# Moving stores to GpSimd's queue, reordering one unit's q loads and changing one PSUM bank in a fused attention and feed-forward kernel

## The chip, the cores and the metric

The kernel runs on one core of a Trainium2 chip (trn2). The metric is the device time of the core in microseconds. Several executions are timed for each kernel, and one of them is traced by the hardware profiler. Engines are named TensorE (PE in the profile, PEld for its weight loads), VectorE (DVE), ScalarE (ACT), GpSimd (POOL) and SyncE (SP, which computes nothing here and only issues DMAs; its queue is SPq). A wait of TensorE is given as its idle time, unless it is said to be counted from start to start. The granted clock is the share of TensorE's full clock that the profile says it was given. A bank is a buffer in PSUM, where the program has the results of matmuls written.

## The reference

```python
def _attn_ref(q, k, v, g_norm):              # (8, 8, 576, 64) each, float32
    kv = np.einsum('bhsd,bhse->bhde', k, v)
    out = np.einsum('bhsd,bhde->bhse', q, kv)
    rms = np.sqrt(np.mean(out * out, axis=-1, keepdims=True) + 1e-06)
    return (out / rms * g_norm).astype(np.float32)
# (B, H, S, D) -> x of (4608, 512), then
def _moe_ref(x, w_in, w_out, s, b):          # w_in (512, 2048), w_out (2048, 512)
    h = x @ w_in
    r = np.maximum(h, 0.0)
    g = s * (r * r) + b
    return (g @ w_out).astype(np.float32)
```

## The kernel before

The 4608 tokens are cut into 36 chunks of 128, and four chunks make a unit: unit `u`, from 0 to 8, has the chunks `4 * u` to `4 * u + 3`. Both large products use a seven-product scheme instead of eight plain ones, for the second product on two levels. While unit `u` is in its first product, the attention of unit `u + 1` is slipped in between: `turn` (transpose q), `product` (q times kv), `row_sum`, `norm`, `turn_x`. Each engine keeps the order in which the program issues its work, so the place of every call matters.

SyncE issues almost every DMA: loads of q, k and v, loads of w_out and its sums into a ring of seven buffers (`pump`), stores of the output, and, in unit 1, 42 stores of parts of w_out (18 as they are, 24 sums or differences), which later units load.

```python
        def parts_of_w(i):                        # unit 1 only, for six of the seven products
            ...
            sub(t1, y12, y11)
            sub(t2, y22, t1)
            sub(t3, y22, y12)
            sub(t4, y21, t2)
            for n, t in enumerate((y11, y21, t2, t3, t1, y22, t4)):
                nc.sync.dma_start(out=w3_dram[i][:, n], in_=t)

        def store(name, j, c, cols=slice(0, DM), queues=(nc.sync, nc.sync)):
            ...                                    # 2 to 4 DMAs a chunk

        def product(with_sum=True):               # q times kv
            ...
                pool, tag = (ps_f, "y") if c == 17 or c > 19 and c % 2 else (ps_a, "x")
                ps = pool.tile([P, NP, P], FP32, name="x_ps", tag=tag)   # ps_a has one buffer, "y" two
```

What unit 3 does for unit 4 (chunks 16 to 19), and the loads of q for chunks 22 and 23 that it issues; keys are (step, place) in the first product, and names of places in the second. `loads_in_parts(5, 1, 4)` cuts the 48 loads of these two chunks into four quarters of twelve.

```python
                first[2, 0] = [*turn_x[:2], turn[2]]
                parts = loads_in_parts(5, 1, 4)
                second["q", 0], second["q", 2] = [parts[2]], [parts[3]]
                first.update({
                    (2, 1): [product[2]],
                    (2, 2): [turn[3], row_sum[2], norm[2], *parts[:2]],
                    (2, 3): [turn_x[2]],
                    (3, 0): [product[3], row_sum[3]],
                    (3, 1): [norm[3]],
                    ...
                })
```

## Time and profile before

| | before |
|---|---|
| time, median of 3 runs | 953.4 us (952.8 to 954.4) |
| span of the traced run | 949.7 us |
| TensorE busy | 931.7 us |
| VectorE, ScalarE, GpSimd busy | 657.3, 204.8, 6.7 us |
| TensorE's named waits, all together | 11.4 us |
| last matmul's end to the end | 5.9 us |

TensorE is busy for nearly the whole span, so only its idle time can be saved.

### The profile page before, as it was taken

To read this page: it belongs to the slowest core of one execution; us is meant where nothing else is said; L and a number is where in the kernel's file an instruction comes from. 1 tells how busy PE (TensorE), PEld (TensorE's weight loads), DVE (VectorE), ACT (ScalarE), POOL (GpSimd) and SP (SyncE) were. 2 spreads that over 40 slices of the span, in tenths; PEclk is the share of its full clock that TensorE was granted. 3 is DMA by queue.
4 is the path that set the end of the run, shared out by engine and by line. 5 is a ranking of instruction groups with operands and counts; after the bars stand their busy time and mean duration, and the time that the engine had idled before them with its cause. 6 is when DMAs were issued, how large, how long until landed. Compare 5 with 4: busy or idle time off the path is not lost.

```text
span 949.7 us, 18256 instructions
## 1 busy us (share of the span) xinstructions
PE 931.7 (98%) x7438; PEld 841.1 (89%) x7438; DVE 657.3 (69%) x1220; ACT 204.8 (22%) x387; POOL 6.7 (1%) x18
## 2 busy tenths in 40 slices
PE   7999999999999999999999999999999999999997
PEld 7888888888888998899879998999889988998997
DVE  2799667486557775777477766776578757774585
ACT  3683132101223012300232013200320033001200
POOL 2000000000000000000000000000000000000000
PEclk9999999999999999999999999999999999999999
DMA  9689727578764767156744774277526720673075
GB/s 262 200 303 255 244 79 197 137 226 255 209 178 121 236 189 230 23 185 214 195 115 127 247 210 108 67 249 216 156 42 222 223 99 12 202 224 118 12 232 168
DMA packets 141220, 165.85 MB, mean 175 GB/s; under 512 B 78161, under 2 KB 94289, under 8 KB 141009
## 3 DMA queue, kind: packets, MB, share of 16 engines
q1 hardware_dynamic: 137072, 162.12, 57.1%
q10 hardware_dynamic: 3744, 2.56, 1.1%
q8 instruction: 59, 0.97, 0.4%
q14 instruction: 25, 0.20, 0.1%
q0 software_dynamic: 320, 0.00, 0.0%
HBM read 136.84 MB, written 27.79 MB: 173 GB/s over the span
## 4 chain that ended last, share of the span: by engine, by line
PE 83%; DVE 6%; DMA 5%; ACT 2%; SPq 2%; issue 1%; DVEq 0%; ACTq 0%
PE x_ps L91 36%; PE y_ps L91 26%; PE z_ps L91 9%; PE t_ps L91 7%; PE x_ps L440 3%; DMA w_sb<-w 2%; PE kv_ps L377 1%; ACT xT L494 1%; DMA w_raw<-in_moe_w_in_dram 1%; SPq L1261 1%; DMA kv_sb<-in_k_dram 1%; DVE a L247 1%; DVE xT L488 1%; DVE a L551 1%; DVE a L637 1%
## 5 line engine op out<-in xcount | busy, mean ns | idle before, releaser
L596 ACT COPY r<-x_ps 128x512 f32<-128x512 f32 x96 | 56.0, 583 | 398.0 <-PE x_ps L91 373.1
L91 PE MATMUL y_ps<-xs,wb 128*128 128x256 f32 x512 | 122.6, 382 | 1.1 <-DVE a L247 1.1
L91 PE MATMUL x_ps<-xs,ws 128*128 128x256 f32 x512 | 122.0, 381 | 0.5
L91 PEld LDWEIGHTS y_ps<-xs,wb 128*128 128x128 f32 x512 | 95.5, 190 | 16.9 <-DVE a L247 3.4
L91 PEld LDWEIGHTS x_ps<-xs,ws 128*128 128x128 f32 x512 | 96.4, 190 | 15.3 <-ACT r L596 2.3
L247 DVE TENSOR_TENSOR a<-y_ps,r 128x512 f32<-128x512 f32 x64 | 43.8, 685 | 76.6 <-ACT r L596 59.8
L91 PE MATMUL x_ps<-xT,wa 128*128 128x256 f32 x384 | 89.8, 380 | 0.1
L91 PEld LDWEIGHTS x_ps<-xT,wa 128*128 128x128 f32 x384 | 72.2, 190 | 10.5 <-ACT xT L494 0.5
L91 PE MATMUL y_ps<-w_sb,sub 128*128 128x128 f32 x560 | 69.5, 275 | 0.1
L91 PEld LDWEIGHTS y_ps<-w_sb,sub 128*128 128x128 f32 x560 | 66.4, 192 | 0.6 <-DVE sub L250 0.3
L551 DVE SCALAR_TENSOR_TENSOR a<-a 128x512 f32<-128x512 f32 x89 | 61.5, 691 | 2.8
L91 PE MATMUL y_ps<-w_sb,a 128*128 128x128 f32 (+1 forms) x416 | 61.2, 295 | 0.5 <-DMA w_sb<-w 0.5
L91 PE MATMUL x_ps<-xT,ws 128*128 128x256 f32 x256 | 60.6, 379 | 1.1 <-ACT r L596 1.1
L91 PE MATMUL z_ps<-xT,wa 128*128 128x256 f32 x256 | 60.5, 379 | 0.0
L91 PEld LDWEIGHTS y_ps<-w_sb,a 128*128 128x128 f32 x416 | 55.4, 192 | 2.9 <-DVE xs L250 0.7
L91 PE MATMUL x_ps<-w_sb,s 128*128 128x256 f32 x256 | 57.8, 380 | 0.0
L91 PEld LDWEIGHTS x_ps<-xT,ws 128*128 128x128 f32 x256 | 48.0, 190 | 7.7 <-ACT r L596 1.5
L91 PE MATMUL t_ps<-w_sb,sub 128*128 128x128 f32 x448 | 54.8, 275 | 0.0
L91 PEld LDWEIGHTS z_ps<-xT,wa 128*128 128x128 f32 x256 | 48.6, 190 | 6.6
L91 PEld LDWEIGHTS x_ps<-w_sb,s 128*128 128x128 f32 x256 | 47.5, 190 | 6.0 <-issue 0.2
L91 PEld LDWEIGHTS t_ps<-w_sb,sub 128*128 128x128 f32 x448 | 52.3, 192 | 0.2
L637 DVE TENSOR_TENSOR a<-a 128x512 f32<-128x512 f32 x25 | 17.3, 690 | 46.5 <-ACT a L631 46.5
(143 smaller groups left out, 1334.9 us busy)
## 6 DMA issues: line engine op xcount, KB each, us to landing
w_sb<-w SPq DMA_DIRECT2D x154, 512.0 KB, 4.6
w_sb<-w SPq DMA_DIRECT2D x42, 256.0 KB, 3.5
w_raw<-in_moe_w_in_dram SPq DMA_DIRECT2D x8, 1024.0 KB, 7.4
w_raw<-in_moe_w_out_dram SPq DMA_DIRECT2D x8, 1024.0 KB, 5.4
w_sb<-in_k_dram SPq DMA_DIRECT2D x48, 144.0 KB, 3.0
w_sb<-in_v_dram SPq DMA_DIRECT2D x48, 144.0 KB, 3.1
w<-sub SPq DMA_DIRECT2D x24, 256.0 KB, 3.8
out_dram<-o SPq DMA_DIRECT2D x92, 64.0 KB, 3.0
```

Source lines behind the costliest of these rows:

```text
L91: nc.tensor.matmul(o, lhsT=lhsT, rhs=rhs, start=start, stop=stop, skip_group_check=True)
L247: nc.vector.tensor_tensor(out=o, in0=a, in1=b, op=ALU.add)
L377: nc.tensor.matmul(ps[r][l * HB : l * HB + HB, i, :], lhsT=kv[l][rows, 0, j, :], rhs=kv[l][rows, 1, j, :], start=(j == 0), stop=(j == R - 1),)
L440: nc.tensor.matmul(ps[32 * p : 32 * p + 32, w, :], lhsT=st["qT"][:, p, 32 * w : 32 * w + 32], rhs=bd_kv[(b if w < 2 else b1) % 2][:, p, :] ...
L488: nc.vector.transpose(out=to, in_=st["xn"].rearrange("p h d -> p (h d)").rearrange("p (c x) -> p c x", c=KC))
L494: nc.scalar.activation(to[:, i], to[:, i], AF.Copy, scale=g_col[:, i : i + 1])
L551: nc.vector.scalar_tensor_tensor(t, t, 0.0, t, ALU.max, ALU.mult)
L596: nc.scalar.copy(st[name], src)
L637: nc.vector.tensor_mul(ga["a21", s], ga["a21", s], ga["a21", s])
L1261: load()
```

## The change

Its intent is to clear SyncE's queue. Output stores and part stores wait for VectorE, and while they stand at the head of an in-order queue, the loads behind them stand too. GpSimd is idle after the start, so it takes the stores. In unit 3 three quarters of q's loads go out together and the last one earlier. Chunk 19's product leaves the one-buffer bank.

```diff
-                pool, tag = (ps_f, "y") if c == 17 or c > 19 and c % 2 else (ps_a, "x")
+                pool, tag = (ps_f, "y") if c > 16 and c % 2 else (ps_a, "x")
@@ parts_of_w
-                nc.sync.dma_start(out=w3_dram[i][:, n], in_=t)
+                nc.gpsimd.dma_start(out=w3_dram[i][:, n], in_=t)
@@
-        def store(name, j, c, cols=slice(0, DM), queues=(nc.sync, nc.sync)):
+        def store(name, j, c, cols=slice(0, DM), queues=(nc.gpsimd, nc.gpsimd)):
@@ the last unit keeps its stores on SyncE and ScalarE
-                store("o2", 1, 4 * u + 3, slice(0, HN))
+                store("o2", 1, 4 * u + 3, slice(0, HN), (nc.sync, nc.sync))
@@ unit 3
-                second["q", 0], second["q", 2] = [parts[2]], [parts[3]]
+                second["q", 0] = [parts[3]]
-                    (2, 2): [turn[3], row_sum[2], norm[2], *parts[:2]],
+                    (2, 2): [turn[3], row_sum[2], norm[2], *parts[:3]],
```

Of the bank's condition only chunk 19 changes: 17 and the odd chunks from 21 on had the y bank already.

## The prediction

> **What bounds the kernel now.** I read the page's busy times and chain first, then TensorE's own waits, then the time-ordered view around each of the longer waits, then SyncE's issue queue over the same stretches. The page, busy times and the chain's shares by engine:
>
> ```profile
> PE 931.7 (98%) x7438; PEld 841.1 (89%) x7438; DVE 657.3 (69%) x1220; ACT 204.8 (22%) x387; POOL 6.7 (1%) x18
> ...
> PE 83%; DVE 6%; DMA 5%; ACT 2%; SPq 2%; issue 1%; DVEq 0%; ACTq 0%
> ```
>
> TensorE is busy for 931.7 of 949.7 us. The change takes no matmul away, so only the 18.0 us of idle time can shrink. About 6 us of it lie after the last matmul, which ends near 943.9 us, and the start-up has its share; the last unit's stores are issued by ScalarE or SyncE after the change too. What is left is in the waits of TensorE (total us, times, longest us):
>
> ```profile
> PE x_ps L440 <- DVE qT L409: 2.0, 2, 1.5
> ...
> PE x_ps L440 <- DVE xn L463: 1.2, 2, 0.6
> ...
> PE y_ps L91 <- DVE a L247: 1.1, 2, 0.8
> PE x_ps L91 <- ACT r L596: 1.1, 1, 1.1
> ...
> PE y_ps L91 <- DMA w_sb<-w: 0.5, 1, 0.5
> ```
>
> The twelve lines of that view sum to 11.4 us. So even a perfect schedule could gain only about 1%. A wait costs about 0.16 us more than its idle time: matmuls of 379 ns start every 216 ns (3.45 us for 16 in the chain), and this overlap is lost too.
>
> The first stall is at 275 us (time-ordered view: start, length, engine; in brackets the idle time before and its releaser):
>
> ```profile
> 268.09 1.97 SPq L822 DMA_DIRECT2D out_dram<-o  x2
> ...
> 271.23 1.83 SPq L1261 DMA_DIRECT2D q_sb<-in_q_dram  x4
> ...
> 276.55 0.71 DVE L409 STREAM_TRANSPOSE qT<-q_sb 128x512 f32<-128x512 f32 x1 [3.71 <-DMA q_sb<-in_q_dram]
> ```
>
> The last four loads of q for chunk 13 are issued only at 271.2 us, behind an output store on the same queue; VectorE idles 3.71 us for them, and chunk 13's product, due at about 275.7, waits 1.5. The queue is full here. From 193.8 to 273.1 us SyncE's issues take about 71 of 79 us: 24.8 for 40 stores of w_out's parts, 5.4 for 8 output stores, 19.0 for 32 loads of q, the rest for ring and k/v loads. (These times hold short waits too.)
>
> The second is in unit 4, after a late quarter of q. SyncE's view, then the full view:
>
> ```profile
> 438.68 7.60 SPq L1261 DMA_DIRECT2D q_sb<-in_q_dram  x12
> 446.38 0.38 SPq L687 DMA_DIRECT2D w_sb<-w  x1
> ...
> 451.93 3.80 SPq L822 DMA_DIRECT2D out_dram<-o  x8
> ...
> 466.56 6.79 SPq L1261 DMA_DIRECT2D q_sb<-in_q_dram  x12
> ```
> ```profile
> 476.22 0.71 DVE L409 STREAM_TRANSPOSE qT<-q_sb 128x512 f32<-128x512 f32 x1 [5.86 <-DMA w_sb<-w]
> ...
> 479.09 1.99 PE L91 MATMUL x_ps<-xT,ws 128*128 128x256 f32 x8 [1.07 <-ACT r L596]
> ...
> 489.16 1.99 PE L91 MATMUL y_ps<-xs,wb 128*128 128x256 f32 x8 [0.81 <-DVE a L247]
> ```
>
> The twelve loads from 466.6 are the last quarter of chunks 22 and 23, queued behind k/v loads and 16 output stores. I read VectorE's 5.86 us as a wait for them, although the view names a ring load: the transpose reads q_sb alone. ScalarE's square root then comes late, holds the copy r behind it, and TensorE waits 1.07 us; ten us later VectorE, still behind, costs 0.81 more. Units 5 to 7 have the same program with q loaded earlier, and no such stall.
>
> The third is chunk 19's product, which shares the one-buffer bank of chunk 18 and must wait until the normalisation has read it:
>
> ```profile
> 387.81 0.69 DVE L463 TENSOR_TENSOR xn<-x_ps,inv 128x512 f32<-128x512 f32 x1
> ...
> 388.65 1.08 PE L440 MATMUL x_ps<-bd_kv,qT 128*32 128x128 f32 x32 [0.64 <-DVE xn L463]
> ```
>
> **What the Trainium skill says.** "DMA: Bandwidth & Descriptors", section "Anatomy of one DMA — SWDGE (gpsimd) path": "any semaphore wait happens on the issuing sequencer before dispatch". The trace agrees: in 190 to 300 us SyncE's queue waits 14.4 us for VectorE's subtractions before part stores, while loads stand behind. The same page, "Issuing engines are not separate DMA queues": issuing from more engines saves only the sequencer's time. That is what is wanted here, since the 16 DMA engines have room (0.79 busy in 190 to 250, 0.64 in 250 to 300). Its "SWDGE vs HWDGE vs iDMA" and "Specifications" say that GpSimd's descriptors are made in software, with about 1 us to the first byte against 0.6. In the trace GpSimd's eight loads of g take it 504 ns each and land in 6.5 us (median), in a start where ScalarE's loads take 6.7 to 8.0: slower than SyncE's stores now (2.4 to 4.9 in the stretch above), but that was under load. "SBUF — State Buffer", section "Who interferes with whom": VectorE locks GpSimd out in two-port copy modes, while an instruction with two SBUF inputs meets only a GpSimd instruction that reads SBUF. From the first moved store on, near 115 us, VectorE has almost only two-input arithmetic and transposes of 0.35 to 0.7 us; no run shows yet whether a descriptor write disturbs them.
>
> **The change, part by part.**
>
> *Part stores to GpSimd (42).* They free about 25 us of SyncE's queue before 273 us. With the 8 output stores it is 30 us, far more than the 3.7 us by which q is late. Stall one goes: 1.5 + 0.16 = 1.7 us. GpSimd needs, at 0.5 to 1 us each (the first measured, the second an estimate with margin for the longer lists), 21 to 42 us over 85 us. It does not become the bound.
>
> *Output stores to GpSimd.* Four a chunk at 0.5 us are 8 us a unit off SyncE. Units 5 to 7 lose nothing to this today (TensorE is busy 99.89 of 100 us in 550 to 650), so beyond unit 4 it is worth nothing. Output tiles have two buffers and are written again a unit later, about 100 us, so a slower landing is hidden.
>
> *Another order of q's loads in unit 3.* Three quarters (36 loads) rather than two go out at 386.7, the last twelve at 438.7 in place of the third, none after. At 12.26 us for 24, 36 end near 405 instead of 399; the first ring load, at 403.8 now, slips about 1 us with six ring buffers ahead of it: harmless. All q is then on chip about 20 us before VectorE asks at 470. Stall two goes whole: (1.07 + 0.16) + (0.81 + 0.16) = 2.2 us. The wait of 0.5 us for a ring load at 449 stays: the load at 446.4 still stands behind twelve loads of q.
>
> *Chunk 19 in the y bank.* It removes 0.64 + 0.16 = 0.8 us, but takes one of two y buffers, so that unit 3's last y product must wait for the sum that reads the previous y. Now:
>
> ```profile
> 398.27 0.68 DVE L247 TENSOR_TENSOR a<-y_ps,r 128x512 f32<-128x512 f32 x1
> 398.40 1.89 PE L91 MATMUL y_ps<-xs,wb 128*128 128x256 f32 x8
> ```
>
> Both move 0.8 us earlier; the sum then ends at 398.95 - 0.8 = 398.15, the matmul would like to start at 397.6: a new wait of 0.55, about 0.6. Net 0.2 us.
>
> Sum: 1.7 + 2.2 + 0.2 = 4.1 us. 953.4 - 4.1 = 949.3 us.
>
> **Rivals.** (1) *Ring buffers wait for software stores.* Part stores read ring tiles, so a ring load in unit 1 waits for their landing (6.7 us in three waits of SyncE now). If GpSimd's stores land 3 us later, the loads do too. Against it: the last one, issued at 227.8 and landed at 233, is needed only near 241. With landings over 8 us later it would cost several us: 951 to 955. (2) *VectorE is slowed or GpSimd starved at the shared port.* If every two-input operation near a store lost some 0.1 us, unit 1 (43.5 us of VectorE in 60) would lose 1 to 2 us: 951. For it: such a lock is documented; against: the forms that lock are rare after 115 us. (3) *The y bank costs nothing, and the ring load at 449 comes in time too*, because less traffic makes q's loads quicker: 0.6 + 0.7 us more, 948. (4) *Nothing moves*, because q's loads are limited by DMA engines: 953. Against: the last four loads were issued at 271.2 us, 1.6 us before VectorE was free for them, and landed within 5.3: the issue was late, not the transfer.
>
> **Range and chances.** The removable idle time caps the gain near 8 us (11.4 less what belongs to the start-up), so faster by over 2% is excluded in practice. The executions before spread by 1.6 us. Rivals 1 and 2 give the upper end, rival 3 and small knock-on gains the lower: 946.8 to 952.2. Slower by over 2% would need 19 us of new waits on TensorE, for which I see no place.
>
> **What would show it.** VectorE's 3.71 us before the transpose near 275 and 5.86 near 476 are gone; TensorE's waits for qT fall to about 0.5 us in all and that for r to none; a wait of about 0.5 us for "a" appears in unit 3's last y product and that for xn of 0.6 goes; 0.5 us for the ring load near 449 stays; units 5 to 7 keep their pace of 100.3 us. Wrong would be: GpSimd issues over 1.5 us each, waits on "sub" or ring buffers in unit 1, VectorE operations longer than 0.69 us, or a later end after the last matmul.

## The result, and the profile after

The changed kernel takes 949.26 us in the median of six runs (947.07 to 951.55), the kernel before 953.27 in six (952.49 to 954.35). The ratio is 0.9957, with a 95% interval of 0.9939 to 0.9976. Ratios here are the mean time of one kernel's runs over that of the other's in the same rounds, so not quite the ratio of the medians. It is faster by 0.4%, clear of noise.

The page of the changed kernel, busy times:

```profile
PE 931.7 (99%) x7438; PEld 841.4 (89%) x7438; DVE 657.1 (70%) x1220; ACT 205.0 (22%) x387; POOL 87.8 (9%) x170
```

TensorE does the same work in a span of 945.3 us. VectorE's total is as before (657.1 against 657.3), so GpSimd's stores did not slow it. GpSimd went from 6.7 to 87.8 us. Its groups (busy time, mean ns of one, idle time before and its releasers):

```profile
L822 POOL DMA_DIRECT2D out_dram<-o x110 | 54.5, 502 | 696.7 <-DVE o L247 537.8 <-DVE o L718 147.9 <-DMA out_dram<-o 8.3
L734 POOL DMA_DIRECT2D w<-w_sb x18 | 13.7, 764 | 18.2 <-DMA w_sb<-w 17.4 <-DMA w<-sub 0.7
L734 POOL DMA_DIRECT2D w<-sub x24 | 13.1, 546 | 48.4 <-DVE sub L250 45.0 <-DMA w<-sub 2.2 <-DVE xs L250 0.9
```

An output store costs GpSimd 502 ns, a part store 546 or 764. The long idle times are the point: GpSimd waits for VectorE, and nothing but other stores waits behind it.

TensorE's waits, the lines that are not of the start:

```profile
PE x_ps L440 <- DVE xn L463: 0.5, 1, 0.5
PE x_ps L440 <- DVE qT L409: 0.5, 1, 0.5
...
PE y_ps L91 <- DVE a L247: 0.3, 1, 0.3
```

The waits for r and for a ring load are gone, that for qT has lost its 1.5 us, that for xn its 0.6, that for a its 0.8. In the time-ordered view chunk 13's last loads are issued at 264.6 us and VectorE turns it without waiting:

```profile
264.62 1.84 SPq L1261 DMA_DIRECT2D q_sb<-in_q_dram  x4
...
273.82 0.70 DVE L409 STREAM_TRANSPOSE qT<-q_sb 128x512 f32<-128x512 f32 x1
...
276.89 1.08 PE L440 MATMUL x_ps<-bd_kv,qT 128*32 128x128 f32 x32
```

In unit 3 chunk 19's product starts without a wait, where it had waited 0.64 us for xn:

```profile
387.49 1.08 PE L440 MATMUL x_ps<-bd_kv,qT 128*32 128x128 f32 x32
```

The same holds in unit 4 for chunks 22 and 23, where VectorE had lost 5.86 us and TensorE had waited for r:

```profile
467.90 1.30 DVE L409 STREAM_TRANSPOSE qT<-q_sb 128x512 f32<-128x512 f32 x2
...
476.01 1.89 PE L91 MATMUL x_ps<-xT,ws 128*128 128x256 f32 x8
```

To see where the time went, the same matmul can be followed in both traces. Starts, in us from the start of the span:

| matmul | before | after | difference | step |
|---|---|---|---|---|
| start-up, first product with the lower half of w_in | 29.67 | 30.66 | +0.99 | +0.99 |
| unit 2, chunk 13's product | 277.40 | 276.89 | -0.52 | -1.51 |
| unit 3, chunk 19's product | 388.65 | 387.49 | -1.16 | -0.64 |
| unit 3, last y product | 398.40 | 397.34 | -1.06 | +0.10 |
| unit 3, product behind the late ring load | 449.53 | 447.85 | -1.68 | -0.62 |
| unit 4, product behind the late r | 479.09 | 476.01 | -3.08 | -1.40 |
| unit 4, y product behind the late VectorE | 489.16 | 485.12 | -4.04 | -0.96 |
| end of the span | 949.73 | 945.30 | -4.43 | -0.39 |

Four stalls give 5.0 us net, the start-up takes back 1.0 of it. The last 0.39 us lie almost wholly behind the last matmul (5.9 us before, 5.5 after). The program of the start-up is the same in both kernels; what differs there is how long the first loads take (the start's waits differ by about as much among the experiments below), so this 1.0 probably belongs to the run and not to the change.

### The profile page after: what moved, and what is told of

Its sections match the earlier page's. It is cut to its first block, busy times and chain, and to the rows that moved or that the text cites.

```text
span 945.3 us, 18302 instructions
## 1 busy us (share of the span) xinstructions
PE 931.7 (99%) x7438; PEld 841.4 (89%) x7438; DVE 657.1 (70%) x1220; ACT 205.0 (22%) x387; POOL 87.8 (9%) x170
## 4 chain that ended last, share of the span: by engine, by line
PE 65%; DVE 2%; ACT 1%; issue 0%
PE x_ps L91 27%; PE y_ps L91 18%; PE t_ps L91 8%; PE z_ps L91 8%; PE x_ps L440 2%; PE kv_ps L377 1%; ACT xT L494 1%; DVE a L637 0%; DVE s L247 0%; DVE a L250 0%; DVE a L551 0%; DVE xT L488 0%; DVE a L247 0%; ACT a L631 0%; ACT r L596 0%
## 5 line engine op out<-in xcount | busy, mean ns | idle before, releaser
L822 POOL DMA_DIRECT2D out_dram<-o x110 | 54.5, 502 | 696.7 <-DVE o L247 537.8
```

Of the source, the lines that this page charges most:

```text
L822: queues[s % 2].dma_start(out=view[b, jj, :, cols], in_=st[name, j][s * w : s * w + w, cols])
```

## The experiments

Theory: the time comes from late q loads at two places and from two smaller stalls, and the two places can be cured in more than one way, because all that matters is what stands in SyncE's queue ahead of a load. Rival: each part of the change cures its own stall only. A second pair concerns the scatter of the changed kernel: clock and start-up, or software-made stores. The first four kernels ran on one chip (kernel before: 951.89 us median of 11 runs), the next three on another (951.56, 11 runs), the last three on a third (951.51, 7 runs). All results were correct.

### The changed kernel again

No edit.

> The changed kernel once more, beside the others. Theory: its scatter (947.1 to 951.6 in six runs) is the granted clock (0.996 to 0.999) and start-up luck, not GpSimd; then the time is 949 +- 2, runs of clock 0.999 near 947, and in the trace the waits near 275, 388, 449 and 476 us are gone again while every VectorE operation keeps its length (two-input 0.68 to 0.69 us). Rival: software-made stores bring random delays; then runs of equal clock differ by over 2 us and the trace shows waits of TensorE that no other run has. Whether the wait of 0.5 us for a ring load near 449 is luck: it may come back here.

Measured: 947.78 us (946.80 to 953.55), ratio 0.9963 (0.9940 to 0.9985). The stalls near 275, 388 and 476 us are gone again. The wait for the ring load near 449 us is back with 0.5 us, so its absence in the first trace was luck. The twelve runs of the changed kernel in both sets sort by granted clock: the six at 0.999 or 1.000 took 946.8 to 948.1 us, the six at 0.996 to 0.998 took 948.6 to 953.6. This shows less than it seems. A half clock can be the result of a wait, as the kernel with output stores alone shows below, and the mean also counts half clock after the last matmul, which costs nothing: all that the first trace of the changed kernel lacks to 1.000 lies there (from 942.5 us on; the last matmul ends at 939.8). Runs of equal clock differ by over 2 us with stores on GpSimd (part stores alone: 950.2 and 955.1 at 0.997) and without (kernel before: 950.5 and 953.5 at 0.998). Runs over 4 us above the kernel's fastest came 4 times in the 24 of the first three kernels with stores on GpSimd (the changed kernel, and the two with one kind of store alone) and once in 47 without (956.12 of the kernel before). So the rival of random delays by GpSimd's stores is not excluded; VectorE's unchanged total, and the one slow run that was traced, speak against it.

### Part stores alone

```diff
-                nc.sync.dma_start(out=w3_dram[i][:, n], in_=t)
+                nc.gpsimd.dma_start(out=w3_dram[i][:, n], in_=t)
```

> Only the 42 stores of w_out's parts go to GpSimd. Theory (the waits near 275 and 476 us can each be removed in two ways): the 25 us of queue freed before 273 us cure the wait near 275, 1.5 to 1.7 us; those near 388 and 476 stay; about 951.7. Rival (each part of the change cures one wait and the output store standing before q's last four loads is what delays them): nothing gained near 275, 953.

Measured: 950.30 us (949.63 to 955.09), ratio 0.9988 (0.9967 to 1.0010). By the medians that is 1.6 us, as the theory has it, but the interval holds 1: the time alone decides nothing. The trace does. TensorE no longer waits near 275 us, nor does VectorE for chunk 13's q, and the waits near 388 and 476 us stand as before (0.6; 1.3 and 0.8).

### Output stores alone

```diff
-        def store(name, j, c, cols=slice(0, DM), queues=(nc.sync, nc.sync)):
+        def store(name, j, c, cols=slice(0, DM), queues=(nc.gpsimd, nc.gpsimd)):
-                store("o2", 1, 4 * u + 3, slice(0, HN))
+                store("o2", 1, 4 * u + 3, slice(0, HN), (nc.sync, nc.sync))
```

> Only the output stores go to GpSimd. Theory: the 16 stores that stand before q's last quarter near 451 to 466 us are 7 to 8 us of queue, and q was late by 5.9, so the waits near 476 us go without any new order: 2.2 us. Near 275 us 8 stores (5.4 us of queue) go against a lateness of 3.7: cured wholly or for the most part, 1 to 1.7 us. The wait near 388 stays. About 949.8. Rival (the order of q's loads is what cures unit 4, and the parts are what cures unit 2): 952 to 953.

Measured: 947.49 us (946.55 to 953.76), ratio 0.9960 (0.9936 to 0.9983). The whole gain is there with no new order of q and no part store moved: in the trace TensorE's waits near 275 and 476 us are both gone, though VectorE still idles 0.99 us for chunk 13's q. The rival falls. Chunk 19's wait of 0.6 us remains and is lost in the noise of the times.

The traced run is the slowest of the six, 953.76 us at a clock of 0.996, and it shows what such a run can be. TensorE waited 1.03 us for VectorE near 101.8 us, in this trace alone and before the first moved store went out at 130.6. The ring load near 449 us came 2.73 us late this time (time-ordered view):

```profile
452.98 2.04 PE L91 MATMUL y_ps<-w_sb,a 128*128 128x128 f32 x8 [2.73 <-DMA w_sb<-w]
```

The view by stretches gives, for each, its length, the busy time and count of TensorE, its weight loads, VectorE, ScalarE and GpSimd, and then TensorE's granted clock, the DMA share and GB/s:

```profile
450.00:452.90 2.90, 0.25 (x3) 0.06 (x1) 1.38 (x4) 0.00 (x0) 1.71 (x4) 1.00 0.85 239
452.90:456.40 3.50, 3.42 (x12) 3.19 (x13) 1.34 (x3) 0.00 (x0) 3.17 (x8) 0.51 0.98 319
```

After the idle time TensorE runs at half clock for 3.4 us and so does 1.7 us less work: a wait of 2.7 us costs 4.4. Another such window of 3.4 us lies in this run's start-up, near 23 us. "TensorE: Matmul & The Clock Gate" of the Trainium skill, section "Part 1: The HAM clock gate", describes this gate: half rate after an idle window of about 3.4 us, in windows that run freely and do not start with the kernel. The traces agree with the length, and differ in that the window before need not be idle. I cut each of the twelve traces into slots of 3.41 us, such that a half-clock stretch starts with a slot. Of the slots at full clock, every one in which TensorE was busy for at most 1.51 us was followed by half clock (0.73 us in the slot from 449.52 above), and none with 1.52 us or more; matmul ends are modelled, so take the limit as about 1.5 us. This fits the start-ups too: three traces have a half-clock window there (this one, the next and the SyncE-only kernel), after slots with 1.25 to 1.51 us; in the nine others the least busy slot of the start-up has 1.56.

### The order of q's loads and the bank alone

The change without its three lines that name GpSimd; all stores stay on SyncE.

> Only q's new order and chunk 19's bank; all stores stay on SyncE. Theory: the waits near 476 us (2.2) and 388 us (0.6 to 0.7) go, the one near 275 us (1.5) stays; about 950.5. Rival: without the freed queue 36 loads in a row hold ring loads back and new waits for w_sb appear near 405 to 412 us; 952 or more.

Measured: 949.76 us (949.00 to 950.59), ratio 0.9973 (0.9959 to 0.9988), 2.1 us by the medians. The waits near 476 and 388 us are gone, that near 275 us stays with 1.1 us, and no wait appears near 405 us behind the 36 loads in a row. The matmul that needs the ring load near 449 us starts 0.68 us late (the view names a subtraction of VectorE that it does not read). So the theory holds, with 0.7 us less gain than expected; the traced run has a half-clock window in its start-up.

### No store on GpSimd, q's loads earlier

The previous kernel, and q for chunks 12 and 13 earlier:

```diff
-            for n, fn in enumerate(loads_in_parts(3, 0, 8)):
-                side.setdefault(6 + n, []).append(fn)
+            for n, fn in enumerate(loads_in_parts(3, 0, 4)):
+                side.setdefault(5 + n, []).append(fn)
```

> No store on GpSimd: q's new order, chunk 19's bank, and the loads of q for chunks 12 and 13 issued from SyncE in four parts one slot earlier instead of eight. Theory (what matters is only that q's loads are not issued late; GpSimd is one way to that): the waits near 275, 388 and 476 us are all gone and the time is that of the changed kernel, about 947.7 on the chip of the first job, give or take 1. Rival (the stores themselves must leave SyncE): the wait near 275 us stays at 1.1 to 1.5, 949.5.

Measured: 949.61 us (948.77 to 950.56), ratio 0.9977 (0.9965 to 0.9988). Neither had it right. The wait near 275 us is gone as the theory says, but the time is that of the rival, because the next load of q is late instead:

```profile
285.89 0.71 DVE L409 STREAM_TRANSPOSE qT<-q_sb 128x512 f32<-128x512 f32 x1 [1.34 <-DMA q_sb<-in_q_dram]
...
286.75 1.08 PE L440 MATMUL x_ps<-bd_kv,qT 128*32 128x128 f32 x32 [1.28 <-DVE qT L409]
```

Chunk 14's loads are issued from 274.5 us on, behind part stores and output stores that now come later in the queue. In this stretch the queue is full, and this reordering only chose which load is late. No other order was tried, so that stores have to leave SyncE there is likely but not shown; in unit 4 an order was enough. My theory was too simple by that distinction. (The ring load near 449 us was 1.1 us late in this run, and the start-up has a half-clock window.)

### The last quarter of q behind the ring load

The changed kernel, with

```diff
-                second["q", 0] = [parts[3]]
+                second["q", 2] = [parts[3]]
```

> The changed kernel with q's last quarter for chunks 22 and 23 issued at the end of unit 3, behind the ring load that TensorE needs near 449 us, instead of ahead of it. Theory: that wait (0.5 us of idle in five of six traces so far, none in one, 2.7 in one, where half clock for 3.4 us came on top) is queueing behind these twelve loads; it goes in every profile, about 0.7 us in the median, and fewer runs have a granted clock of 0.996. The last quarter is still in time, since no output store stands ahead of it (none of the waits near 476 us in the kernel that moved only the output stores). About 947. Rival: the ring load is late by itself, or the wait near 476 us returns (2.2 us).

Measured: 946.75 us (946.12 to 948.36), ratio 0.9950 (0.9938 to 0.9962). The wait near 449 us is gone, that near 476 us has not come back, and the slowest of six runs is 948.36, where the changed kernel had 951.55 and 953.55. The granted clocks are 0.997 to 0.999. (Of the six earlier traces, the wait had 0.50 to 0.53 us in three, 0.68 in the one with the order and the bank alone, 2.73 in one, and was absent in one.) That the ring load was late because twelve loads of q stood ahead of it is shown by this trace and by both traces of the next kernel, which keeps the edit and has no such wait. That this also removes the slow runs is likely: none of the 14 runs of these two kernels is over 2.3 us above its kernel's fastest, against 2 of 12 over 4 us.

### Three more waits

The previous kernel, and

```diff
-            3: [product[0]],
-            4: [turn[1]],
+            3: [product[0], turn[1]],
@@ unit 2
-                (3, 3): [turn[3]],
-            second = {3: [product[3]], ...
+            second = {0: [turn[3]], 3: [product[3]], ...
@@ product
+                if c == 7:
+                    pool, tag = ps_t, "t"
```

> The previous one with three more waits attacked in the same manner: chunk 9's turn of q one slot earlier, ahead of four subtractions (wait of 0.5 near 214 us), chunk 15's turn after unit 2's last sum instead of before it (0.3 near 300 us), chunk 7's product in a transpose bank rather than in the one-buffer bank (0.5 near 132 us). Each wait costs 0.16 more than its idle time, so 0.6 + 0.4 + 0.6 = 1.6 us at most: 945.5. Rival: the turns only move VectorE's lateness elsewhere (new waits of TensorE for a, or or qT), and the time equals that of the previous kernel.

Measured: 944.24 us (943.76 to 945.26, 4 runs), ratio 0.9922 (0.9909 to 0.9935). That is 2.5 us under the previous kernel by the medians, 1.6 expected; all three waits are gone from the trace and no others came after the start. The three edits were not run one by one, and the 0.9 us more than expected is not explained. What TensorE still waits for by name lies wholly in the first 35 us. This version beats both kernels.

> The best version once more on this chip: a ratio of 0.991 to 0.9935 to the kernel before, no wait of TensorE of over 0.2 us between 35 and 940 us, and no run over 947 us.

Once more, on the third chip: 945.31 us (944.14 to 945.88, 4 runs), ratio 0.9927 (0.9908 to 0.9947), as expected and again without a named wait of TensorE after the start.

### Part stores on ScalarE

```diff
-                nc.gpsimd.dma_start(out=w3_dram[i][:, n], in_=t)
+                nc.scalar.dma_start(out=w3_dram[i][:, n], in_=t)
```

> The changed kernel with the 42 part stores issued by ScalarE instead of GpSimd; output stores stay on GpSimd. Theory (what matters is that the stores leave SyncE's queue; in unit 1 ScalarE is 15% busy): the same as the changed kernel, a ratio of 0.995 to 0.997 to the kernel before, no wait near 275 us. Rival: stores that wait for VectorE's subtractions or for a ring load block ScalarE's own copies, and TensorE gets new waits for r or xT between 190 and 255 us, 1 to 3 us.

Measured: 963.33 us (961.97 to 964.03), ratio 1.0116 (1.0100 to 1.0133): slower than the kernel before. The rival is right, and its 1 to 3 us are far too little. The stores that wait for VectorE's subtractions block ScalarE's own work, which is short but urgent:

```profile
209.59 0.59 ACT L427 COPY qT<-qT_ps 128x512 f32<-128x512 f32 x1 [12.11 <-DMA w<-sub]
```

TensorE's waits for qT, r and a come to 12.7 us here (two lines of qT with 4.7 and 1.6, r 4.7, a 1.7; 0.5 of it the changed kernel has too). Half-clock windows from 238.3 us (6.8 us long, the first 1.1 of them still idle) and from 265.6 us (3.4) cost about half of the 9.1 us that TensorE works in them, 4.5 us more.

### All moved stores on ScalarE

The previous edit, and the default of `store` is `(nc.scalar, nc.scalar)`.

> The changed kernel with all moved stores issued by ScalarE. Theory: at the end of each unit 16 output stores of some 0.45 us, the last of them waiting for VectorE's last sum, stand in ScalarE's queue ahead of the copy r that the next unit's third product needs 1.7 us after its first; each of the units 2 to 6 then loses 1 to 3 us, 953 to 962 in all, with waits of TensorE for r at each start of a unit. Rival: the stores are issued early enough and ScalarE is as good a place as GpSimd, ratio 0.996.

Measured: 1016.63 us (1014.09 to 1018.33), ratio 1.0676 (1.0650 to 1.0702). The mechanism is the expected one, at the start of every unit, but several times larger:

```profile
470.60 11.08 ACTq L822 DMA_DIRECT2D out_dram<-o  x16
...
481.72 0.59 ACT L596 COPY r<-x_ps 128x512 f32<-128x512 f32 x1 [46.67 <-DMA w_sb<-in_v_dram]
...
482.35 3.78 PE L91 MATMUL x_ps<-xs,ws 128*128 128x256 f32 x8 [4.98 <-ACT r L596]
```

Sixteen output stores hold ScalarE's queue for 11.1 us, TensorE waits 5 us for the copy r, and then runs at half clock: eight matmuls take 3.78 us instead of 1.89. I had counted 0.45 us a store and no half clock.

## Why the prediction was right

The total was right: 949.3 us predicted, 949.26 measured. Its terms, against the table of the result:

- **Chunk 13's q (1.7 us).** Right: 1.5 measured. Both kinds of store were named as cures, and either alone suffices, as the two kernels with one kind each show. With neither, the one earlier order that was tried only hands the lateness to chunk 14. So the full queue was the cause, as the sum of its issues had suggested. (The first moved store goes out at 128.9 us, not "near 115", which changes nothing here.)
- **Chunks 22 and 23's q (2.2 us).** Right: 1.40 and 0.96 measured. The reading that VectorE waited for q and not for the ring load that the view named is shown by the kernels that remove the wait. But the credit went to the new order alone; the output stores by themselves do it too, so these parts overlap.
- **Chunk 19's bank (0.2 us net).** The removal was right (0.64), the new wait was not: it took 0.10, not 0.6. The step that failed is that "unit 3's last y product must wait for the sum that reads the previous y". In the changed kernel the product starts before that sum has ended:

```profile
396.50 0.69 DVE L463 TENSOR_TENSOR xn<-x_ps,inv 128x512 f32<-128x512 f32 x1
397.11 0.68 DVE L247 TENSOR_TENSOR a<-y_ps,r 128x512 f32<-128x512 f32 x1
...
397.34 1.97 PE L91 MATMUL y_ps<-xs,wb 128*128 128x256 f32 x8
```

  The sum ends at 397.79, after the matmul's start. The bank that this sum reads was therefore not the one that the y product got, and of the two buffers only chunk 19's is left; its last reader, xn, had ended at 397.19. I had taken the two buffers to alternate. That they are handed out in the order in which the program releases them fits this, but was not tested by itself.
- **The ring load near 449 us (nothing).** Right for the kernel: it is late by 0.5 us again in the second trace of the changed kernel. In the first trace it was not, which made this run 0.6 us better than the sum. The twelve loads of q ahead of it took 7.6 us to issue in the trace before and 6.7 in the first one after:

```profile
437.69 6.72 SPq L1261 DMA_DIRECT2D q_sb<-in_q_dram  x12
444.52 0.38 SPq L687 DMA_DIRECT2D w_sb<-w  x1
```

  In the trace before, one of these issues took 1.42 us instead of 0.43, and in the slow run with output stores alone one took 1.75. This is not the whole of it: with part stores alone no issue was long and the load was still 0.50 us late. Why a single issue sometimes takes so long stays open.
- **The rivals.** Ring buffers that wait for GpSimd's stores did not reach TensorE: SyncE's waits for part stores grew from 6.7 to 22.0 us, hidden as reckoned. VectorE was not slowed. GpSimd's issue cost lay in the assumed 0.5 to 1 us.
- **What the prediction did not have.** The profiled run's gain is 5.0 us in the stalls, of which a slower start-up took 1.0 back. And the median of the changed kernel lies some 2 us above its fastest run, because some runs lose several us; none of its own slow runs was traced, and half clock after a wait, as in the slow run with output stores alone, is the likely reason but not shown. That these deviations from the sum of 4.1 nearly cancel in the median is luck; the terms were each within 0.7 us.

The order of size is worth noting. TensorE's idle time of 18 us was known from the first page, so nothing near 2% was to be had, and the kernel with every named wait after the start removed still gains only 0.7 to 0.8%.

## What to carry to other kernels

When an engine that bounds a kernel stalls for a load, look first at what stands ahead of that load in the issuing engine's in-order queue: a store that waits for a late result holds every load behind it, and where the queue is full, reordering can just move the lateness to the next load, as it did here. Put waiting stores on an engine that has nothing else to do; on an engine with short urgent work the same stores cost 16 to 69 us here (963.33 and 1016.63 against 947.78, where the kernel before took 951.5 and 951.9). A matmul stream that idles for under 3 us can cost more than the idle time, through half-clock time after it, so a wait that is small in the median may be behind the slow runs.

## What the Trainium skill lacked or had wrong

- "DMA: Bandwidth & Descriptors", section "Anatomy of one DMA — SWDGE (gpsimd) path": it calls descriptor generation small and variable and gives no time for which an issue holds GpSimd. Here an issue held GpSimd 502 ns (output stores of 64 or 128 KB), 546 ns (256 KB parts from their own tile) or 764 ns (the same size, cut out of a ring tile). Landing took 3.9 us against 3.0 from SyncE for the 64 KB stores, 5.2 against 3.8 for the parts from their own tile, 6.3 against 4.4 for those out of the ring.
- The same page, "Issuing engines are not separate DMA queues": it calls the sequencer time saved by more issuing engines usually small relative to the DMA itself. That holds here for a single store (0.5 us to issue, 3 to 4 to land), but it misleads: the queue time of many stores, with their waits, was the gain (about 4 us with output stores alone), and the choice of engine was worth more: some 16 us between GpSimd and ScalarE for the parts alone. No page draws out what a DMA that waits costs the compute of the engine that issues it.
- "TensorE: Matmul & The Clock Gate", "Part 1: The HAM clock gate": an idle window of about 3.4 us is named for half rate. Here the window need not be idle: half clock followed every slot of 3.41 us at full clock in which TensorE was busy for at most 1.51 us, and no other, in twelve traces. So idle times of 2.61, 2.72 and 2.73 us were each followed by 3.4 us at half clock (the kernels with all stores on ScalarE and with output stores alone), and one of 1.5 us (unit 2 of the kernel before, with 2.06 us busy in its slot) by none.
- No page gives a figure for how much longer than usual a single issue on SyncE can take: loads of q had medians of 0.43 and 0.45 us and a longest of 1.42 and 1.67 (its two lines in the trace before).
